# Clustered attention and a top-2 mixture of experts: the experts' first layer on float16 halves, scaled by powers of two found on the chip, with new first steps and a last list made by matmuls

## The chip, the cores and the metric

The program runs on one core of one Trainium2 chip. The metric is the device time of one execution in microseconds (us); the figure for a kernel is the median over its runs. The engines are TensorE (PE, with PEld for its weight loads), VectorE (DVE), ScalarE (ACT), GpSimd (POOL) and SyncE (SP, which here only sends DMAs).

## The reference, cut to what matters

```python
def _attn_ref(q, k, v, centroids):            # q, k, v: 4 x 8 x 768 x 64; centroids: 8 x 16 x 64
    q_n, k_n, c_n = (t / (norm(t) + 1e-06) for t in (q, k, centroids))
    q_assign = np.argmax(np.einsum('bhsd,hcd->bhsc', q_n, c_n), axis=-1)
    k_assign = np.argmax(np.einsum('bhsd,hcd->bhsc', k_n, c_n), axis=-1)
    mask = q_assign[:, :, :, None] == k_assign[:, :, None, :]
    scores = np.where(mask, q @ k.T / 8, -1e9)
    return softmax(scores) @ v

def _moe_ref(x, w_gate, w_noise, noise, w1, w2):   # x: 3072 x 512; w1: 8 x 512 x 1024; w2: 8 x 1024 x 512
    noisy_logits = x @ w_gate + np.log1p(np.exp(x @ w_noise)) * noise
    top2_w = softmax of the two largest, top2 their experts
    for e in range(8):
        for k in range(2):
            mask = top2[:, k] == e
            h = np.maximum(x[mask] @ w1[e], 0.0)
            out[mask] += top2_w[mask, k, None] * (h @ w2[e])
```

All inputs are float32; x is the attention's output, heads side by side.

## The kernel before, in words

**Attention.** 16 head pairs (4 batches of 4), each pair 12 steps: two heads, six blocks of 128 keys. A step makes scores of one block against 768 queries (`scores`, lines 485 and 486: matmuls into PSUM, then `Exp` on ACT), splits the weights into a bfloat16 upper part and a float16 rest (`split_p`, line 497, on POOL, in the last steps on DVE), and four steps later multiplies with v (`values`, lines 514 to 520, 16-bit matmuls with 65 or 64 columns). Queries and keys stand as an fp32r upper half and rest in two big tiles, `A` and `B`, three of each in turn. They are filled by DMAs from `hl` (`b_place`, line 426, ten a pair, 2.25 MB), with the one-hot cluster rows from `mk` (`b_mask`, four DMAs) and the negated row maximum from `nt` (`b_negT`). `b_max` (lines 454 and 457) finds the row maximum: 24 matmuls a pair, each with one DVE reduction out of PSUM. For pair 0 `nt` goes out once for each head, later once a pair.

**The order.** It is written by hand in `attention`: `at(step, f)` puts each function into a third of a step, and the table `AT` holds the steps. Within one engine's queue everything then runs in that order, so a function that waits holds up what stands behind it on its engine. SP sends nearly all loads and copies. PSUM has a ring of six buffers (`ps`).

**Experts.** After each batch the gate (`g_gate`) picks two experts a token and writes each token's number and weight to a list in DRAM by indirect DMAs (`g_list`, line 703, twelve a batch, on POOL). For each expert up to 832 rows (`CAP`, seven blocks of 128 or 64) are gathered by the list (`gather_x`), transposed (`turn_x`) and split into halves (`halves`, lines 905 and 906: ACT copies to the upper half, DVE subtracts for the rest). w1 and w2 are loaded through the staging tile `stg` (three buffers) and split alike. `layer1` (line 953) does for each of 8 blocks of F and 4 of D three matmuls (upper by upper, upper by rest, rest by upper), each over two parts of 416 columns: 192 matmuls an expert; `layer2` (line 992) does 24 matmuls of 512 columns a block of rows. For expert 0 the first four blocks of rows come from the lists of batches 0 to 2 alone (`lst0`, 512 columns); the other three (320 columns) wait for the last batch's list. All of layer 1 and 2 is fp32r.

Of the kernel before, what the change touches and what calls it, by code (L numbers as in the profile page):

```python
# [27 lines left out]
    first={'place': -2.333, 'sims': [-3.333, -2.667], 'sum': [-2.333, -2.333], 'max1': -2.333, 'ge': -2.333, 'max2': -2.333, 'eq': -1.333, 'mask': 1.667, 'bmask': 4.0, 'ky': -2.333, 'split': [-5.333, -5.0, -5.333, -4.0], 'bmax': [10.0, 17.0], 'neg': [17.667, 24.667], 'negT': [20.667, 27.667]},  # L28
    L=4, qk=-20.667, v=-8.667,
    vscale=-0.667, vsplit=10.667, vstep=1.0, split=[-4.667, -3.667, -4.0, -3.333], place=-0.667,  # L30
    sims=[-3.0, 2.0], sum=[2.333, 3.333], max1=3.333, ge=3.667, max2=4.333, eq=4.667, mask=5.667, bmask=6.0,
# [3 lines left out]
    vd=[1, 1, 2, 3, 4, 5], sec=-7.333, qf=-8.667,  # L35
    fv={'v': -2.333, 'vscale': -1.0, 'am': 0.0, 'amstep': 0.333, 'vsplit': 3.0, 'vstep': 2.0},
    thr=0.333, bsec=0.0)
# [6 lines left out]
class Kernel:  # L44
# [17 lines left out]
    def constants(self):  # L62
# [55 lines left out]

    def ps(self):
        return self.psum.tile([128, 512], F32, name="ring", bufs=6)  # L120

    def rnorm(self, n, r):
# [4 lines left out]
        nc.scalar.preload_act_table(AF.Exp)  # L127
# [5 lines left out]
    def centroids(self):  # L133
# [4 lines left out]
        nc.gpsimd.dma_start(c1, self.cent.rearrange("h c d -> (h c) d"))  # L138
# [7 lines left out]
    def c_turn(self):  # L146
# [4 lines left out]
        hi = self.pre.tile([128, HC], F32R, name="chi")  # L151
        lo = self.pre.tile([128, HC], F32R, name="clo")
        nc.scalar.activation(hi, p[:, :HC], AF.Copy)
        nc.vector.tensor_tensor(lo, p[:, :HC], hi, op=OP.subtract)
        for s in range(2):
            r = slice(64 * s, 64 * s + 64)
            for src, dst, c0 in ((hi, self.wh, 64 + 32 * s), (lo, self.wh, 80 + 32 * s)):
# [3 lines left out]
    def attention(self, ctx):  # L161
# [27 lines left out]
        for p in range(NP):  # L189
# [864 lines left out]
```

## Time and profile before

| | us |
|---|---|
| time, median of 3 runs | 1123.19 (1122.86 to 1123.75) |
| the profiled execution | 1116.65 |
| its span | 1114.9 |
| PE busy | 1056.4 (95%) |
| DVE, ACT, POOL busy | 612.7, 476.8, 559.2 |
| layer 1, PE (line 953, 1536 matmuls) | 290.3 |
| layer 2, PE (line 992, 1152 matmuls) | 273.7 |
| attention, end of the last values | some 482 |

The span is cut into the start (to about 60 us), the attention's steady steps, its end with the first expert's weights (440 to 482), the last gate and expert 0 (to some 560), and experts 1 to 7. PE is busy in nearly all of it, so the reading goes by where PE waits and by what each of its matmuls takes. A matmul's own duration in the trace holds its latency; what counts in a dense run is the distance from one start to the next, that is, busy time over count.

### The profile page before, as it was taken

Reading aid. Unit: us, or ns where it says so; the run is one execution under the profiler, and the core shown is the slowest. Engines: PE = TensorE matmul, PEld = TensorE weight load, DVE = VectorE, ACT = ScalarE, POOL = GpSimd, SP = SyncE. Lnnn points to the kernel's source line nnn. Section 1 sums busy time; section 2 is a strip of 40 time slices with the busy share of each in tenths; the row PEclk is TensorE's granted clock in tenths of the full one; section 3 lists DMA queues with packets and bytes.
Section 4 is the critical chain, followed back from the end, with each engine's and each line's share of the span. In section 5 each row is a group of like instructions: output and inputs, shape, how many; then the busy total and the mean of one; then the engine's idle time right before and its main releaser. Section 6 shows DMA issues by size and latency. Waiting matters only on the chain. (4 is left out here: it accounts for less than half of the span.)

```text
span 1114.9 us, 22318 instructions
## 1 busy us (share of the span) xinstructions
PE 1056.4 (95%) x8658; PEld 943.2 (85%) x8658; DVE 612.7 (55%) x1326; ACT 476.8 (43%) x961; POOL 559.2 (50%) x608
## 2 busy tenths in 40 slices
PE   4799999999999999889899999999999999999995
PEld 4589888888889888778889899898898898998983
DVE  5867786878687869964254333344244334433411
ACT  3476767676767675732233223133132232330300
POOL 4767775789678968606433351343233413522311
PEclk9899999999999999999899999999999999999998
DMA  8856767566757653132244342352153233523200
GB/s 232 179 140 153 176 157 203 143 171 156 206 143 178 155 151 106 39 135 82 86 126 157 133 136 78 126 176 84 67 168 125 94 112 134 161 68 106 76 32 32
DMA packets 87327, 144.46 MB, mean 130 GB/s; under 512 B 13945, under 2 KB 65529, under 8 KB 86706
## 3 DMA queue, kind: packets, MB, share of 16 engines
q1 hardware_dynamic: 71922, 106.45, 35.8%
q0 software_dynamic: 13712, 36.42, 9.7%
q8 instruction: 69, 1.13, 0.4%
q10 hardware_dynamic: 1584, 0.13, 0.1%
q14 instruction: 40, 0.33, 0.1%
HBM read 78.21 MB, written 26.53 MB: 94 GB/s over the span
## 5 line engine op out<-in xcount | busy, mean ns | idle before, releaser
L953 PE MATMUL ring<-xT,w1t 128*128 128x416 f32 (+2 forms) x1536 | 290.3, 350 | 0.0
L497 POOL TENSOR_TENSOR pl<-pe 128x768 f16<-128x768 f32 x173 | 252.2, 1473 | 72.3 <-ACT pe L486 69.5
L953 PEld LDWEIGHTS ring<-xT,w1t 128*128 128x128 f32 x1536 | 282.7, 188 | 6.6 <-DVE xT L906 0.3
L992 PE MATMUL ring<-w2t,hT 128*128 128x512 f32 x1152 | 273.7, 394 | 0.0
L992 PEld LDWEIGHTS ring<-w2t,hT 128*128 128x128 f32 x1152 | 214.5, 189 | 43.3
L486 ACT ACTIVATE pe<-ring,l 128x384 f32<-128x384 f32 x384 | 201.1, 578 | 54.2 <-PE ring L485 48.8
L1005 POOL DMA_INDIRECT out<-yo,lst x56 | 65.6, 1171 | 237.3 <-DVE yo L1001 187.5
L457 DVE TENSOR_REDUCE aux<-ring 128x1 f32<-128x384 f32 x192 | 108.0, 563 | 70.6 <-PE ring L454 66.0
L485 PE MATMUL ring<-A 128*128 128x384 f32 x384 | 141.3, 368 | 0.3 <-DVE aux L457 0.3
L963 DVE SCALAR_TENSOR_TENSOR hT<-ring,hT 128x416 fp32r<-128x416 f32 (+3 forms) x128 | 66.2, 554 | 124.1 <-ACT hT L962 124.1
L962 ACT ACTIVATE hT<-ring 128x416 fp32r<-128x416 f32 (+3 forms) x128 | 56.8, 488 | 181.0 <-PE ring L953 180.9
L932 POOL DMA_INDIRECT xg<-xs,lst x56 | 65.7, 1173 | 130.9 <-PE ring L943 105.1
L485 PE MATMUL ring<-B 128*128 128x384 f32 x384 | 129.4, 337 | 1.8 <-DMA B<-nt 1.8
L1001 DVE SCALAR_TENSOR_TENSOR yo<-ring,lst,xt 128x512 f32<-128x512 f32 (+1 forms) x49 | 36.7, 750 | 166.6 <-PE ring L992 145.8
L454 PE MATMUL ring<-A 128*128 128x384 f32 x384 | 110.5, 363 | 7.5 <-ACT pe L486 2.6
L905 ACT ACTIVATE xT<-ring 128x512 fp32r<-128x512 f32 (+1 forms) x56 | 31.0, 565 | 176.8 <-PE ring L943 176.8
L457 DVE TENSOR_REDUCE mm<-ring 128x1 f32<-128x384 f32 x192 | 105.2, 548 | 0.0
L514 PE MATMUL av<-vv,pe 128*128 128x65 f16 x1152 | 98.2, 196 | 4.5 <-DVE xt L528 4.4
L514 PEld LDWEIGHTS <-pe 128*128 128x128 bf16 x1152 | 80.5, 99 | 19.9 <-issue 11.8
L516 PE MATMUL av<-vv,pe 128*128 128x64 f16 x1152 | 97.2, 193 | 0.0
L454 PEld LDWEIGHTS ring<-A 128*128 128x128 f32 x384 | 71.0, 194 | 20.3 <-ACT pe L486 9.8
L516 PEld LDWEIGHTS <-pe 128*128 128x128 bf16 x1152 | 78.8, 99 | 0.3
(174 smaller groups left out, 1354.9 us busy)
## 6 DMA issues: line engine op xcount, KB each, us to landing
stg<-in_moe_w SPq DMA_DIRECT2D x64, 512.0 KB
A<-hl SPq DMA_DIRECT2D x30, 384.0 KB
B<-hl SPq DMA_DIRECT2D x30, 384.0 KB
vt<-in_v SPq DMA_DIRECT2D x8, 768.0 KB
out<-zt SPq DMA_DIRECT2D x12, 512.0 KB
xs<-xt SPq DMA_DIRECT2D x4, 1536.0 KB
A<-hl SPq DMA_DIRECT2D x60, 96.0 KB
B<-hl SPq DMA_DIRECT2D x30, 192.0 KB
```

The source lines that it names most:

```text
L454: nc.tensor.matmul(t, A[:, 0, s, j * 128:j * 128 + 128], A[:, 1, s, n * 384:n * 384 + 384], start=True, stop=True)
L457: nc.vector.tensor_reduce(o, t, axis=X, op=OP.max, negate=True)
L485: nc.tensor.matmul(t, M[:, 1 - qi, s, ks], M[:, qi, s, ns], start=not qi, stop=bool(qi))
L486: nc.scalar.activation(pe[:, n], t, AF.Exp, bias=self.l64[:, 0:1], scale=self.scale)
L497: (nc.vector if last else nc.gpsimd).tensor_tensor(lo, pe, hi, op=OP.subtract)
L514: nc.tensor.matmul(av[:, j, :], ph[:, js], vv[:, hh, kj, 64:129], start=(kc == 0 and j == 0), stop=False, skip_group_check=True)
L516: nc.tensor.matmul(av[:, j, :64], ph[:, js], vv[:, hh, kj, 0:64], start=False, stop=False, skip_group_check=True)
L932: self.nc.gpsimd.indirect_dma_start(out=xg[:r], out_offset=None, in_=self.xs[:n], in_offset=bass.IndirectOffsetOnAxis(ap=self.entry(e, t)[ ...
L953: nc.tensor.matmul(p, self.w1t[:, wi, c, f * 128:f * 128 + 128], self.xT[:, xi, c, n0:n1], start=(i == 0), stop=(i == 3 * ND - 1))
L963: nc.vector.scalar_tensor_tensor(h1, x, 0.0, h0, op0=OP.max, op1=OP.subtract)
L992: nc.tensor.matmul(p, self.hT[:, hi, f, t * 128:t * 128 + 128], self.w2t[:, wi, f], start=(i == 0), stop=(i == 3 * NF - 1))
L1005: i = nc.gpsimd.indirect_dma_start(out=self.out, out_offset=bass.IndirectOffsetOnAxis(ap=en[:r, 0:1], axis=0), in_=yo[:r], in_offset=None, ...
```

## The change

Four things, all in one diff.

1. `w1t` and `xT` become float16. Both are multiplied by a power of two first: the largest absolute value over all partitions is found on the chip (`x_max` from the maxima of v that the attention has anyway, `max_w1` for each expert), spread by a transpose, a maximum and a matmul with a row of constants (`scale_a`, `scale_b`), cut to its exponent by a bit mask, and its reciprocal scales both halves (`scaled_halves`). The product of the two powers (`ce`) is multiplied into the tokens' weights (`eff`, `weight`).
2. `stg` gets six buffers; w1 is loaded earlier (`prep_w1`), and its maxima are taken when it lands.
3. The last batch's list isn't written and read back: `upper`, `l_hot` and `l_sum` make it by one-hot comparisons and 12 float32 matmuls, added to what the earlier batches wrote (`lst`, now loaded sooner).
4. The first steps: other steps in `AT`, centroid halves written straight to `wh`, the loads of the second q and k and of v later, the gate's loads on SP, the `Exp` table after the first `nt`, and clears of `xg` on POOL.

```diff
-    first={... 'mask': 1.667, 'bmask': 4.0, ... 'bmax': [10.0, 17.0], 'neg': [17.667, 24.667], 'negT': [20.667, 27.667]},
+    first={... 'mask': -1.0, 'bmask': -1.0, ... 'bmax': [3.667, 22.667], 'bstep': [1.0, 0.667], 'neg': [9.0, 26.667], 'negT': [9.333, 27.333]},
-    vd=[1, 1, 2, 3, 4, 5], sec=-7.333, qf=-8.667,
-    fv={'v': -2.333, 'vscale': -1.0, 'am': 0.0, ...},
-    thr=0.333, bsec=0.0)
+    vd=[1, 1, 2, 3, 4, 5], sec=-6.0, qf=-4.0, place1=4.333,
+    fv=[{'v': -5.0, 'vscale': 13.0, 'am': 24.333, ...}, {'v': 9.0, 'vscale': 11.667, ...}],
+    thr=0.333, bmax1=14.667, bstep1=0.5)
...
-        nc.gpsimd.dma_start(c1, self.cent.rearrange("h c d -> (h c) d"))
+        nc.sync.dma_start(c1, self.cent.rearrange("h c d -> (h c) d"))
...
-        hi = self.pre.tile([128, HC], F32R, name="chi")
-        lo = self.pre.tile([128, HC], F32R, name="clo")
-        nc.scalar.activation(hi, p[:, :HC], AF.Copy)
-        nc.vector.tensor_tensor(lo, p[:, :HC], hi, op=OP.subtract)
...
-                nc.vector.tensor_copy(dst[r, :, c0:c0 + C],
-                                      src.rearrange("p (h c) -> p h c", c=C)[r])
+            nc.scalar.activation(hi, src, AF.Copy)
+            nc.vector.tensor_tensor(lo, src, hi, op=OP.subtract)
...
+        for i in range(2):
+            at(z - 45 + 2 * i, self.x_scale, i)
+            at(z - 13 + i, self.w1_scale, 0, i)
+        at(z - 46, self.x_max)
         for i in range(4):
-            at(z - 24 + i if i < 3 else z - 9, self.load_w1, 0, i)
+            at(z - 24 + i, self.load_w1, 0, i)
+            at(z - 19 + i, self.max_w1, 0, i)
             at(z - 10 + 2 * i, self.split_w1, 0, i)
...
-        self.w1t = self.mw.tile([128, 2, self.DM // 128, self.F], F32R, name="w1t")
+        self.w1t = self.mw.tile([128, 2, self.DM // 128, self.F], F16, name="w1t")
...
-        self.xT = mo.tile([128, 2, ND, CAP], F32R, name="xT")
+        self.xT = mo.tile([128, 2, ND, CAP], F16, name="xT")
...
-        for i in range(2 * NJ):
-            self.g_list(b, i)
+        self.l_hot(0)
         for i in range(4):
             if i >= 2:
                 self.load_w2(0, i)
-            self.split_w2(0, i)
             if f < NF:
                 self.layer1(0, f, [A])
                 f += 1
-        self.load_list(1)
+            if i < 2:
+                self.l_sum(i)
+            if i < 1:
+                self.l_hot(i + 1)
+            self.split_w2(0, i)
...
+    def l_hot(self, h):
+        self.hot = self.mo.tile([128, NJ, 128], F32, name="hot", bufs=1)
+        nc.vector.tensor_tensor(self.hot, self.low[:, NJ * h:NJ * h + NJ, None].to_broadcast([128, NJ, 128]),
+                                self.lower[:, None, :].to_broadcast([128, NJ, 128]), op=OP.is_equal)
+        self.ent = self.mo.tile([128, n, 2, 2, W], F32, name="ent", bufs=1)
...
+    def l_sum(self, h):
+        for i in range(NJ):
+            nc.tensor.matmul(self.lps, self.hot[:, i], ent[:, i], start=(h == 0 and i == 0), stop=(h == 1 and i == NJ - 1))
+        if h == 1:
+            nc.vector.tensor_tensor(self.idx, self.lps[:, :W], ls[:, :, 0], op=OP.add)
+            nc.vector.tensor_tensor(self.lsw, self.lps[:, W:], ls.bitcast(F32)[:, :, 1], op=OP.add)
...
+    def scaled_halves(self, dst, st, s):
+        self.nc.scalar.activation(dst[:, 0], st, AF.Copy, scale=s)
+        self.nc.vector.scalar_tensor_tensor(dst[:, 1], st, s, dst[:, 0], op0=OP.mult, op1=OP.subtract)
+    def scale_a(self, m):
+        nc.tensor.transpose(t[:k, :128], m, self.ident)
+        nc.vector.reduce_max(g[:k], t[:k, :128], axis=X)
+    def scale_b(self, g, f, p, s):
+        nc.tensor.matmul(t, f, g, start=True, stop=True)
+        nc.vector.tensor_scalar(p.bitcast(I32), t.bitcast(I32), 0x7F800000, None, op0=OP.bitwise_and)
+        nc.vector.reciprocal(s, p)
+    def max_w1(self, e, c):
+        self.nc.vector.tensor_reduce(self.wm[:, c:c + 1], self.stg[1, c], axis=X, op=OP.max, apply_absolute_value=True)
...
-        self.stg[1, c] = st = self.mw.tile([128, self.F], F32, name="stg", bufs=3)
+        self.stg[1, c] = st = self.mw.tile([128, self.F], F32, name="stg", bufs=6)
...
-            self.nc.vector.memset(xg, 0.0)
+            self.nc.gpsimd.memset(xg, 0.0)
```

How it moves instructions, at three places. Names of tiles are those of the program; after each comes the shape. First SP's queue near the start, before: the mask copies of pair 0 (`mk` into `A_142`), the copies of pair 1 (`xt` into `A_143` and `B_146`), its mask, a load of v, and the first `nt` of pair 0.

```order
L426 DMA A_142<-mk 16x2x384 x4
L426 DMA A_143<-xt 64x4x384
L426 DMA A_143<-xt 32x2x384 x2
L426 DMA B_146<-xt 64x4x384
L426 DMA B_146<-xt 32x4x384
L426 DMA A_143<-xt 64x4x384
L426 DMA A_143<-xt 32x2x384 x2
L426 DMA B_146<-xt 64x4x384
L426 DMA B_146<-xt 32x4x384
L426 DMA A_143<-mk 16x2x384 x4
L301 DMA vt<-in_v 128x4x384
L426 DMA B_145<-nt 2x6x128
```

And after, from the same mask copies (now into `A_151`): two loads of q and k, the first `nt`, then the copies of pair 1.

```order
L455 DMA A_151<-mk 16x2x384 x4
L323 DMA qk<-in_q 128x4x384
L323 DMA qk<-in_k 128x4x384
L455 DMA B_154<-nt 2x6x128
L455 DMA A_152<-xt 64x4x384
L455 DMA A_152<-xt 32x2x384 x2
L455 DMA B_155<-xt 64x4x384
L455 DMA B_155<-xt 32x4x384
L455 DMA A_152<-xt 64x4x384
L455 DMA A_152<-xt 32x2x384 x2
L455 DMA B_155<-xt 64x4x384
L455 DMA B_155<-xt 32x4x384
```

The first `nt` of pair 0 has moved from behind pair 1's copies and mask to ahead of them; the second `nt` of pair 0 stands behind pair 2's copies, as before.

Next PE's queue at the start, before, behind the sums of pair 0: the matmul that spreads v's maxima, then pair 1's transposes, then the mask's transposes (the one-hot tile `oh_148`).

```order
L388 MATMUL ring<-csum,sm 128x64 x6
L322 LDWEIGHTS vones
L322 MATMUL ring<-vm,vones 128x4
L323 LDWEIGHTS ones
L323 MATMUL ring<-tiny,ones 128x4
L352 MATMUL ring<-ident,qk 128x128 x12
L418 LDWEIGHTS oh_148
L418 MATMUL ring<-identb,oh_148 128x128
```

After:

```order
L417 MATMUL ring<-csum,sm 128x64 x6
L447 LDWEIGHTS oh_157
L447 MATMUL ring<-identb,oh_157 128x128
L447 LDWEIGHTS oh_157
L447 MATMUL ring<-identb,oh_157 128x128
```

The mask's transposes now follow the sums; v's maxima have gone behind the first scores, and pair 1's transposes behind the mask.

Last DVE's queue at the end of the attention, before: the row maxima of the last pair (`aux`, `mm`) and the splits of the attention weights that DVE takes over from POOL (`pl`).

```order
L457 TENSOR_REDUCE mm<-ring 128x1
L457 TENSOR_REDUCE aux<-ring 128x1
L457 TENSOR_REDUCE mm<-ring 128x1
L497 TENSOR_TENSOR pl<-pe 128x768
L457 TENSOR_REDUCE aux<-ring 128x1
L457 TENSOR_REDUCE mm<-ring 128x1
L497 TENSOR_TENSOR pl<-pe 128x768
```

After:

```order
L486 TENSOR_REDUCE mm<-ring 128x1
L1042 TENSOR_REDUCE wm<-stg 128x1
L486 TENSOR_REDUCE aux<-ring 128x1
L486 TENSOR_REDUCE mm<-ring 128x1
L1042 TENSOR_REDUCE wm<-stg 128x1
L526 TENSOR_TENSOR pl<-pe 128x768
L486 TENSOR_REDUCE aux<-ring 128x1
L486 TENSOR_REDUCE mm<-ring 128x1
L1042 TENSOR_REDUCE wm<-stg 128x1
```

Between them now stand the maxima of the first expert's w1 (`wm`), four in all.

## Rows read from the trace of the kernel before

**Rows 1.** The page: span, busy times, and DVE's tenths in 40 slices.

```profile
span 1114.9 us, 22318 instructions
PE 1056.4 (95%) x8658; PEld 943.2 (85%) x8658; DVE 612.7 (55%) x1326; ACT 476.8 (43%) x961; POOL 559.2 (50%) x608
...
DVE  5867786878687869964254333344244334433411
```

**Rows 2.** Windows: us, busy PE, PEld, DVE, ACT, POOL (instructions), PEclk, DMA share, GB/s.

```profile
0.00:20.00 20.00, 8.88 (x33) 7.66 (x33) 10.56 (x34) 5.56 (x10) 11.87 (x21) 1.00 0.93 264
20.00:30.00 10.00, 5.60 (x34) 5.08 (x34) 5.70 (x11) 4.94 (x10) 0.64 (x1) 1.00 0.55 126
30.00:40.00 10.00, 6.77 (x28) 5.62 (x28) 7.70 (x16) 3.76 (x7) 8.95 (x7) 0.66 0.88 172
40.00:60.00 20.00, 17.91 (x79) 12.73 (x79) 18.07 (x42) 7.79 (x17) 13.17 (x8) 0.91 0.87 202
...
440.00:450.00 10.00, 10.00 (x146) 9.19 (x145) 9.58 (x21) 6.35 (x13) 8.82 (x10) 1.00 0.02 3
...
530.00:540.00 10.00, 7.41 (x27) 6.00 (x28) 1.72 (x3) 1.58 (x3) 3.18 (x6) 0.66 0.25 95
```

**Rows 3.** Groups by shape, layer 1 on PE: count, busy us, mean ns, idle before.

```profile
L953 PE MATMUL ring<-xT,w1t 128*128 128x416 f32 x1344 | 253.7, 350 | 0.0
...
L953 PE MATMUL ring<-xT,w1t 128*128 128x512 f32 x96 | 22.3, 391 | 0.0
...
L953 PE MATMUL ring<-xT,w1t 128*128 128x320 f32 x96 | 14.2, 309 | 0.0
```

**Rows 4.** Timeline of PE: start us, us, line, operation, shapes, count.

```profile
62.84 0.35 PE L520 MATMUL av<-vv,pl 128*128 128x65 f16 x6
...
63.57 0.50 PE L418 MATMUL ring<-identb,oh 128*128 128x128 bf16 x6
...
729.37 6.92 PE L953 MATMUL ring<-xT,w1t 128*128 128x416 f32 x36
```

**Rows 5.** Groups by shape: the 16-bit weight loads of line 520.

```profile
L520 PEld LDWEIGHTS <-pl 128*128 128x128 f16 x1152 | 48.0, 98 | 0.0
```

**Rows 6.** Groups by shape: the nearest rows for what is added.

```profile
L497 POOL TENSOR_TENSOR pl<-pe 128x768 f16<-128x768 f32 x173 | 252.2, 1473 | 72.3 <-ACT pe L486 69.5 <-PE av L520 1.8
...
L457 DVE TENSOR_REDUCE aux<-ring 128x1 f32<-128x384 f32 x192 | 108.0, 563 | 70.6 <-PE ring L454 66.0
...
L388 PE MATMUL ring<-csum,sm 128*128 128x64 f32 x192 | 26.4, 277 | 1.6 <-ACT sm L378 1.6
...
L311 DVE TENSOR_REDUCE vm<-vt 128x2 bf16<-128x768 f32 x16 | 14.9, 943 | 0.0
...
L931 DVE MEMSET xg<- 128x512 f32 x4 | 1.9, 485 | 0.2
```

**Rows 7.** Waits of PEld, 400 to 570 us: total, times, longest.

```profile
PEld L514 <- DVE xt L528: 5.5, 3, 3.7
```

**Rows 8.** Timeline around the wait for gathered rows.

```profile
532.59 2.58 PE L943 MATMUL ring<-ident,xg 128*128 128x128 f32 x12 [3.54 <-DMA xg<-xs,lst]
...
535.10 7.24 PE L992 MATMUL ring<-w2t,hT 128*128 128x512 f32 x24
```

**Rows 9.** Timeline of the first steps, all engines.

```profile
21.20 0.56 DVE L409 TENSOR_TENSOR oh<-ring,km 128x384 bf16<-128x384 f32 x1
...
26.22 0.57 PE L418 MATMUL ring<-identb,oh 128*128 128x128 bf16 x6
...
30.45 2.93 SPq L426 DMA_DIRECT2D A<-xt  x3
...
41.05 3.60 SPq L426 DMA_DIRECT2D A<-mk  x4
...
60.18 0.67 SPq L426 DMA_DIRECT2D B<-nt  x1
...
65.76 0.45 PE L485 MATMUL ring<-B 128*128 128x384 f32 x1 [1.46 <-DMA B<-nt]
```

More of the change, by code (lines that the diff above doesn't have):

```diff
@@ L321, in total @@
             T["t"] = self.ps()[:, :4]
[L322 removed]
+            nc.tensor.matmul(T["t"], self.vones, self.vm[:, 2 * b + g], start=True, stop=False)
             nc.tensor.matmul(T["t"], self.ones, self.tiny, start=False, stop=True)
@@ L727, in entry, with weight @@
     def entry(self, e, t):
-        return self.lst0[:, t] if e == 0 and t < self.TA else self.lst[:, e, t]
+        i = e * self.T + t
+        return self.lst0[:, t, 0:1] if e == 0 and t < self.TA else self.idx[:, i:i + 1]
+    def weight(self, e, t):
+        return self.we[e % 2][:, t:t + 1]
     def rows(self, t):
@@ L815, in tail @@
         if n < E:
-            for i in range(3):
-                self.load_w1(n, i)
             if e == 0:
@@ L832, in tail @@
             if n < E:
-                if t == t0:
-                    self.split_w1(n, 0)
-                    self.load_w1(n, 3)
-                if t == t0 + 1:
-                    for i in range(1, 4):
+                if e:
+                    self.prep_w1(n, t - t0 + 5)
+                for i in range(4):
+                    if t == t0 + (max(i, 1) if e else min(i, 1)):
                         self.split_w1(n, i)
@@ L857, in extra @@
         with tc.If(self.more > 0):
+            for j in range(self.NJ):
+                for k in range(2):
+                    nc.gpsimd.indirect_dma_start(
+                        out=self.tbl, out_offset=bass.IndirectOffsetOnAxis(ap=self.addr[:, j, k:k + 1], axis=0),
+                        in_=self.rec[:, j, k, :], in_offset=None)
             with tc.For_i(0, E) as e:
@@ L860, in extra @@
                     self.load_w1(e, i)
+                    self.max_w1(e, i)
+                for i in range(2):
+                    self.w1_scale(e, i)
+                for i in range(4):
                     self.split_w1(e, i)
@@ new lines, in w1_scale, with eff @@
+    def w1_scale(self, e, i):
+        if i == 0:
+            self.wg_ = self.scale_a(self.wm)
+        else:
+            self.pw1, self.sw1 = (self.mw.tile([128, 1], F32, name=n, bufs=1) for n in ("pw1", "sw1"))
+            self.scale_b(self.wg_, self.fw, self.pw1, self.sw1)
+            self.ce = self.mw.tile([128, 1], F32, name="ce", bufs=2)
+            self.nc.vector.tensor_tensor(self.ce, self.pw1, self.px, op=OP.mult)
+    def eff(self, e, t0, t1):
+        if t0 == 0:
+            self.we[e % 2] = self.mw.tile([128, self.T], F32, name="we", bufs=2)
+        w = self.lst0.bitcast(F32)[:, t0:t1, 1] if e == 0 and t1 == self.TA else self.lsw[:, e * self.T + t0:e * self.T + t1]
+        self.nc.vector.tensor_scalar(self.we[e % 2][:, t0:t1], w, self.ce, None, op0=OP.mult)
@@ L996, in layer2 @@
         en = self.entry(e, t)
-        wt = en.bitcast(F32)[:r, 1:2]
+        wt = self.weight(e, t)[:r]
         if e == 0:
```

135 lines of the change are left out of this document (107 added, 28 removed).

## The prediction

> **What bounds the kernel now.** I read the page first: of a span of 1114.9 us TensorE (PE) is busy for 1056.4 [rows 1], so a gain must come from PE's own work or from the stretches in which it has none. The windows show where those lie [rows 2]: in the first 60 us PE is busy for 8.88 + 5.60 + 6.77 + 17.91 = 39.2 us, so it stands idle for 20.8, and its granted clock falls to 0.66 in one stretch. There the DMA engines are 55 to 93% busy, and in 40 to 60 us VectorE (DVE) works 18.07 of 20 us. A second hole lies at 530 to 540 us (PE 7.41 of 10, clock 0.66). Before the experts DVE is the full engine (9.58 of 10 us at 440 to 450). Behind 540 us PE never waits, so a nanosecond off a matmul there is a nanosecond off the end, and work added on ACT, DVE or POOL there is free as long as it fits beside PE.
>
> **Layer 1 on float16.** The groups by shape [rows 3] give PE time for each matmul: 253.7 us/1344 = 188.8 ns at 416 columns, 22.3/96 = 232.3 at 512, 14.2/96 = 147.9 at 320. At the full clock of 2.4 GHz the columns alone are 173.3, 213.3 and 133.3 ns, so each fp32r matmul carries 14 to 19 ns above its columns. A run of 36 says the same, (6.92 - 0.35)/35 = 187.7 ns [rows 4]. The 16-bit matmuls of the attention show what is left of that: six with 128 columns take (0.50 - 0.22)/5 = 56 ns, 2.7 above their 53.3; six with 65 columns take (0.35 - 0.19)/5 = 32 ns, 5 above their 27.1 [rows 4]; each has a weight load of its own ahead of it, and that load's 98 ns [rows 5] don't show in the spacing. No wide 16-bit matmul is in the trace, so I bound it: at best 2.7 above the columns, at worst as now. I take 3.5, near the rows with a load for each matmul: 176.8, 216.8, 136.8 ns. Gain: 12.0 x 1344 = 16.1 us, 15.5 x 96 = 1.5, 11.1 x 96 = 1.1, together **-18.7 us** (-19.5 to 0). Number and width of the matmuls stay.
>
> The Trainium skill's page "TensorE: Matmul & The Clock Gate" (Weight-path perf modes) has a fast weight load that 128 columns of a type other than FP32 get and FP32 doesn't; by that the 14 ns would be load time and go, which makes the same sum as mine, and the trace has only the narrow matmuls to show it.
>
> **Scales.** Each expert's w1, and x once, gets a transpose and a float32 matmul with one column: 9 pairs. The nearest float32 rows are the sums of line 388, two records for each matmul, 26.4/192 = 0.137 us a record [rows 6]. Three records a pair: 27 x 0.137 = **+3.7 us** on PE (1 to 6). What the answers need (maximum, bit mask, reciprocal on DVE) stands one list of matmuls ahead, so I cost PE's wait at nothing in the experts; if that cover failed, some 0.5 us each. The w1 maxima there, 4 an expert at about 0.943 x 1024/768 = 1.26 us [rows 6], lie on a DVE that is busy for three to five tenths of nearly every slice there (the last row of [rows 1]); the changed splits keep their number. w1 is fetched earlier into six buffers in place of three, so its loads have more time.
>
> **End of the attention.** Here the cover fails. The order of DVE shows four maxima of w1 between the row maxima of the last head pair: 4 x 1.26 = 5.0 us, and seven small operations, about 1.1, where DVE was 96% busy [rows 2]. Four clears of 0.485 us [rows 6] leave DVE for POOL, which only writes there: -1.9. Net 4.2 us, and PE in that stretch already waits for DVE for 5.5 us [rows 7]. DVE's own gaps can take little: **+3.5 us** (0 to 6). Queued behind a maximum are the row maxima, whose PSUM buffers PE needs.
>
> **The last list by matmuls.** Now PE waits 3.54 us for gathered rows that come of twelve list writes on POOL, a list load and a gather; then it runs cold: 12 transposes take 2.58 us and the 24 matmuls behind them 7.24 [rows 8]. At 232.3 ns the 24 are 5.6 + 0.2, so 1.5 is lost there, and of the 2.58 about half (1.3). All 6.3 us go, as the new chain gives indices before layer 2 begins, one list of 72 matmuls ahead of their use. In their place come 12 float32 matmuls of 112 columns, 24 records: 3.3 us at 0.137, up to twice that as they have more columns than 64; I take 3.5. The first six need a comparison of 672 and one of 768 elements (DVE, about 0.9 us each by its maxima of 768) and four POOL products of 168 elements, 1.47 x 168/768 = 0.32 each and a fixed part [rows 6]: some 3.3 us behind the addresses, with one layer 1 pass of 2.6 us for cover but hidden only in part, since DVE also evicts. I take a wait of 1.9. Sum: -6.3 + 3.5 + 1.9 = **-0.9 us** (-4 to +3).
>
> **First steps.** In the order, the mask of head pair 0 now follows its sums at once; before, its transposes began at 26.22 though the one-hot rows were done at 21.20 + 0.56 = 21.8 [rows 9]. With the centroids written straight into place (2 to 3 us of casts gone, of which I take 1.7, since the same DVE also makes the splits) they begin near 20.1, and SP sends the mask at some 21.8, 6 us sooner. Maxima of the first half only: 12 reductions of 0.563 us [rows 6] from about 26 us, so the first `nt` goes out near 33.5 and the first scores start some 9 us earlier than now. But SP is in order, and now this `nt` stands ahead of pair 1's copies: those took from 30.45 to 41.05, 10.6 us at a DMA share of 0.87 or more, and the mask 3.6 [rows 2, 9]. So: pair 1's copies 34.2 to 44.8, mask to 48, pair 2's copies to 58.6, and only then the second half's `nt`, sent at 60.18 now. It lands now at 65.76, behind two loads of q and k that SP sends just ahead of it; these follow it in the new order, so I give it 3 us: 61.6. PE blocks on it at step 6, as now. Gain 65.8 - 61.6 = 4.2, less four maxima matmuls put off: **-4 us**. Ends: -9 if the copies are not held by bandwidth, +2 if the `nt` takes as long as before. The gate's loads, moved from ACT's queue to SP's, stand ahead of pair 3's copies, which wait for PE anyway: about 2.7 us by the 0.9 of a mask copy, nine steps before use, nothing.
>
> **How the numbers follow.** -18.7 + 3.7 + 3.5 - 0.9 - 4.0 = -16.4 us. The profiled execution took 1116.65 (1114.9 of span), 6.5 under the median of the runs, 1123.2; I take the difference from the median: 1106.8, said as **1106.5**.
>
> **Rivals.**
> (1) The start is freed: copies overlap more than I think, -9 in place of -4, and the list gains its 4: 1096 to 1101. For it speaks the idle 20.8 us; against, the DMA shares.
> (2) The start gives nothing and DVE's maxima cost 6: 1112 to 1119. SP's order speaks for it.
> (3) Slower: the weight load, now an instruction of its own, is not hidden behind a wide matmul. Then 128 columns are added to each: (416 + 128)/2.4 = 226.7 ns, +37.9 x 1344 = +50.9; 512 columns +34.4 x 96 = 3.3, 320 columns +38.8 x 96 = 3.7. With the other terms (+2.3) the time is 1183. It decides from 12 ns of unhidden load a matmul. Against it: 32 and 56 ns spacing with loads between [rows 4, 5]. The same page of the Trainium skill (Part 3, The mechanism) says that loads overlap running matmuls only in other row groups, which would be this case; the trace does not agree, with 32 ns.
> (4) The 14 ns are not the type's: layer 1 stays, 1123.2 + 2.3 = 1125.5.
> (5) 16-bit pairs go faster than a column a cycle. If 512 columns took 131 ns and 416 106.4, layer 1 would lose (188.8 - 106.4) x 1344 = 110.7 and 16 on the others: 999. No row of the trace has a matmul under its columns at 2.4 GHz. That 131 is the figure of the Trainium skill, same page, "Back-to-back issue gap", for a stream of load and matmul; the rows here side with the other formula there, columns/2.4 plus 2.5 ns.
> That the type is not changed at all I leave out: the tiles of x and w1 are declared float16, and the order lists loads apart from matmuls.
>
> **Chances.** Forecast (1101 to 1112) 0.60; (1) 0.17; (2) 0.13; (3) 0.04; (4) 0.04; (5) 0.02. Within 0.2% is 2.2 us, about what a measurement of this kernel tells from no change. Faster: 0.60 + 0.17 + 0.12 + 0.02 = 0.91; same 0.03 (the tail of 2 and half of 4); slower 0.06. The range 1096 to 1116 takes in the forecast, most of (1) and two thirds of (2).
>
> **What would show it.** Layer 1 groups at 176 to 178 ns for 416 columns (right) or 188 and 227 (4, 3); no PE wait for gathered rows at 530 us; DVE over 95% and PE waits for it at 440 to 480; PE's wait for `nt` of the second half near 61 us. The prediction is wrong if layer 1's PE time is not near 271 us, or if PE's idle time in the first 60 us changes by more than 9.

## The result, and the profile after

| | before | after |
|---|---|---|
| median of 6 runs each, taken together | 1123.03 (1120.22 to 1123.75) | 1112.04 (1107.88 to 1112.76) |
| the profiled execution, its span | 1116.65, 1114.9 | 1111.9, 1110.1 |
| layer 1, PE | 290.3 | 274.4 |

The ratio is 0.9891 (0.9872 to 0.9910): the kernel is 11.0 us faster, and 5.5 us slower than forecast. In a later series on one chip the ratio was 0.9934 (0.9918 to 0.9949), 1110.89 against 1118.45. There the kernel before, unchanged, had a median 4.6 us lower than here, and the kernel after one about 1 us lower; the last section shows what the profiles have of it.

The page's first lines and groups of PE by shape (group, operation, shapes, count, busy time and mean ns, idle time before); they answer [rows 1, 3, 6]:

```profile
span 1110.1 us, 22397 instructions
...
PE 1044.8 (94%) x8709; PEld 815.9 (74%) x8709; DVE 660.2 (59%) x1412; ACT 484.3 (44%) x962; POOL 542.2 (49%) x598
...
L1105 PE MATMUL ring<-xT,w1t 128*128 128x416 f16 x1344 | 237.7, 339 | 0.2 <-DVE xT L1010 0.2
...
L1105 PE MATMUL ring<-xT,w1t 128*128 128x512 f16 x96 | 23.1, 400 | 0.0
...
L1105 PE MATMUL ring<-xT,w1t 128*128 128x320 f16 x96 | 13.6, 299 | 0.0
...
L1029 PE MATMUL ring<-gmax,fw 4*128 4x1 f32 x16 | 3.0, 256 | 0.0
...
L1020 PE MATMUL ring<-ident,wm 128*4 128x128 f32 x8 | 2.3, 289 | 2.0 <-DVE wm L1042 2.0
```

The 416 columns are 0.1 ns off the forecast of 176.8: 237.7 / 1344 = 176.9 ns. The scales' two lines are 5.3 us, and 6.0 with x's own pair.

Windows of after, answering [rows 2]:

```profile
0.00:20.00 20.00, 9.03 (x43) 8.12 (x44) 11.46 (x35) 5.35 (x11) 18.97 (x26) 0.94 0.78 211
20.00:30.00 10.00, 8.35 (x36) 7.47 (x34) 6.54 (x14) 3.18 (x7) 5.93 (x4) 0.61 0.84 228
30.00:40.00 10.00, 5.03 (x29) 4.83 (x29) 7.92 (x17) 4.28 (x7) 0.00 (x0) 0.73 0.49 99
40.00:60.00 20.00, 15.84 (x109) 12.55 (x107) 16.26 (x37) 10.44 (x21) 10.77 (x9) 0.97 0.87 187
...
456.00:460.00 4.00, 0.48 (x2) 0.51 (x3) 3.90 (x8) 0.24 (x1) 3.53 (x6) 0.73 0.03 3
460.00:464.00 4.00, 4.00 (x35) 3.50 (x35) 3.26 (x9) 2.59 (x5) 3.33 (x6) 0.50 0.05 8
...
500.00:520.00 20.00, 17.85 (x99) 9.30 (x97) 14.28 (x46) 5.12 (x9) 5.53 (x9) 0.91 0.15 56
530.00:540.00 10.00, 10.00 (x48) 8.27 (x47) 0.94 (x2) 0.00 (x0) 2.16 (x4) 1.00 0.14 54
```

PE's idle time in the first 60 us is 60 - 38.25 = 21.8, where it was 20.8: the holes of the start have not closed. The hole at 530 is gone, and a new one stands at 456 to 460, with the granted clock at its lower level (0.50, that is 1.2 GHz) behind it. PE's longest waits from 440 to 560 us (engine, tile and line, what it waited for, total, times, longest) name the places; `nm` is the negated row maximum of the last pair, `xt` the attention's output, `wm` the maxima of w1, `hot` the one-hot rows of the list:

```profile
PE ring L500 <- DVE nm L495: 4.2, 1, 4.2
PE av L543 <- DVE xt L557: 2.9, 2, 1.8
PE ring L1020 <- DVE wm L1042: 2.0, 1, 2.0
PE ring L761 <- DVE hot L745: 1.8, 1, 1.8
```

The second was there before, and longer; the waits for `wm` and `hot` are new, and that for `nm` was 1.3:

```profile
PE av L514 <- DVE xt L528: 4.4, 2, 3.4
```

Starts of the same matmuls in the profiles, in us, read from timelines of PE ("again" is a later profile; "float16 alone" and "no scales" are experiments below):

| | scores 0 | step 6, behind `nt` | step 30 | step 164 | step 184 | layer 1 | its 320 columns | expert 1 | last matmul |
|---|---|---|---|---|---|---|---|---|---|
| before | 49.5 | 65.8 | 116.6 | 427.8 | 462.8 | 490.2 | 542.2 | 574.1 | 1101.0 |
| before, again | 50.3 | 66.1 | 117.0 | 428.8 | 470.1 | 494.8 | 546.7 | 578.6 | 1105.5 |
| after | 41.9 | 62.0 | 117.5 | 429.3 | 470.4 | 495.2 | 546.6 | 580.1 | 1095.1 |
| after, again | 41.9 | 62.1 | 117.1 | 428.3 | 469.6 | 494.5 | 544.5 | 578.0 | 1093.1 |
| float16 alone, again | 50.4 | 66.1 | 117.0 | 430.7 | 465.6 | 494.0 | 541.7 | 572.6 | 1083.6 |
| no scales, again | 41.0 | 61.7 | 115.3 | 426.9 | 461.8 | 485.9 | 537.2 | 568.1 | 1079.5 |

### The profile page after: what moved, and what is told of

Read it like the earlier page. It is cut to its first block, busy times and chain, and to the rows that moved or that the text cites. A ratio compares the mean times of both kernels' runs of the same rounds, so it can differ in the third digit from the quotient of the medians.

```text
span 1110.1 us, 22397 instructions
## 1 busy us (share of the span) xinstructions
PE 1044.8 (94%) x8709; PEld 815.9 (74%) x8709; DVE 660.2 (59%) x1412; ACT 484.3 (44%) x962; POOL 542.2 (49%) x598
## 4 chain that ended last, share of the span: by engine, by line
PE 72%; DVE 11%; issue 8%; POOL 2%; ACT 2%; DMA 2%; SPq 1%; POOLq 0%; DVEq 0%; ACTq 0%
PE ring L1105 20%; PE ring L1144 19%; PE ring L514 9%; PE ring L483 5%; PE av L543 3%; PE av L549 2%; PE av L545 2%; PE ring L1095 2%; DVE aux L486 2%; PE ring L402 2%; PE ring L381 2%; DMA A<-mk 1%; DVE mm L486 1%; PE ring L417 1%; POOL out L1157 1%
## 5 line engine op out<-in xcount | busy, mean ns | idle before, releaser
L1105 PE MATMUL ring<-xT,w1t 128*128 128x416 f16 (+2 forms) x1536 | 274.4, 340 | 0.2 <-DVE xT L1010 0.2
L1105 PEld LDWEIGHTS <-w1t 128*128 128x128 f16 x1536 | 149.9, 98 | 121.8 <-issue 5.4
L1157 POOL DMA_INDIRECT out<-yo,idx x52 | 62.8, 1208 | 233.6 <-DVE yo L1153 144.3
L1153 DVE SCALAR_TENSOR_TENSOR yo<-ring,we,xt 128x512 f32<-128x512 f32 (+1 forms) x49 | 36.8, 750 | 156.5 <-PE ring L1144 133.7
L1115 DVE SCALAR_TENSOR_TENSOR hT<-ring,hT 128x416 fp32r<-128x416 f32 (+3 forms) x128 | 66.1, 553 | 80.3 <-ACT hT L1114 74.4
L1084 POOL DMA_INDIRECT xg<-xs,idx x52 | 54.2, 1041 | 116.8 <-PE ring L1095 100.3
L1009 ACT ACTIVATE xT<-ring,sx 128x512 f16<-128x512 f32 (+1 forms) x56 | 35.7, 653 | 150.5 <-PE ring L1095 150.5
```

Source lines behind the costliest of these rows:

```text
L1105: nc.tensor.matmul(p, self.w1t[:, wi, c, f * 128:f * 128 + 128], self.xT[:, xi, c, n0:n1], start=(i == 0), stop=(i == 3 * ND - 1))
L1115: nc.vector.scalar_tensor_tensor(h1, x, 0.0, h0, op0=OP.max, op1=OP.subtract)
L1157: i = nc.gpsimd.indirect_dma_start(out=self.out, out_offset=bass.IndirectOffsetOnAxis(ap=en[:r], axis=0), in_=yo[:r], in_offset=None, boun ...
```

## Experiments

Each was timed beside the kernel before, in three series: (S1) before 1123.8, (S2) before 1117.87 on another chip, (S3) before 1118.45 on the chip of S1. The kernel after itself was timed in the first comparison and in S3 alone, so what S1 and S2 say of it compares across series. An issue gap is idle time of PE in which it waits for nothing that the profile shows. Theories: T1, the terms of the prediction; T2, float16 alone gives all of the gain and the scaling that it needs eats a large part; the first steps give nothing.

**Float16 alone.** The kernel before with

```diff
-        self.w1t = self.mw.tile([128, 2, self.DM // 128, self.F], F32R, name="w1t")
+        self.w1t = self.mw.tile([128, 2, self.DM // 128, self.F], F16, name="w1t")
-        self.xT = mo.tile([128, 2, ND, CAP], F32R, name="xT")
+        self.xT = mo.tile([128, 2, ND, CAP], F16, name="xT")
```

> The kernel before with one thing changed: w1t and xT are float16 (no scaling, so the rests lose low bits; nothing else is left out). Theory A (the spacing of the columns): layer 1's PE time falls from 290.3 to 271 us and the kernel is 18 to 19 us quicker than before, 1104 to 1105; no rest of the kernel moves. Theory B (as the trace of after shows, 274.4): some 16 us, 1107, where a cold clock in expert 0 eats the gain of the 512 and 320 columns. Theory C: half or less, under 9 us, because the quicker layer 1 meets its evictions or loads and waits.

Measured in S1: 1105.10, 18.7 us less than before, ratio 0.9838 (0.9812 to 0.9864).

> The kernel before with float16 alone (no scaling), again, now beside the others. Against the kernel without scales it lacks the new first steps, the list by matmuls and the earlier loads of w1. Theory A: first steps 0, list 1.0: 1 us slower than the kernel without scales. Theory B: as the prediction, first steps 4 and list 0.9: 5 us slower. Theory C: its end of the attention, as that of the kernel before, has PE's issue gaps and the half clock behind them in most executions, which the kernel without scales has not shown: 5 to 7 us slower, all of it between step 180 and step 184.

Measured in S3: 1099.06, 19.4 less, 0.9824 (0.9808 to 0.9841). Layer 1's groups of that run:

```profile
L953 PE MATMUL ring<-xT,w1t 128*128 128x416 f16 x1344 | 237.6, 339 | 0.0
...
L953 PE MATMUL ring<-xT,w1t 128*128 128x512 f16 x96 | 21.0, 379 | 0.0
...
L953 PE MATMUL ring<-xT,w1t 128*128 128x320 f16 x96 | 13.2, 299 | 0.0
```

That is 176.8, 218.8 and 137.5 ns and 271.8 us in all, where 271 was forecast; both series agree with theory A of the first expectation. With the type the layer's weight loads became shorter, from 188 to 98 ns each (before, then after):

```profile
L953 PEld LDWEIGHTS ring<-xT,w1t 128*128 128x128 f32 x1536 | 282.7, 188 | 6.6 <-DVE xT L906 0.3
L1105 PEld LDWEIGHTS <-w1t 128*128 128x128 f16 x1536 | 149.9, 98 | 121.8 <-issue 5.4
```

In after the 512 columns have 23.1 us, since some of them run at the lower clock behind the wait for `hot` at 510 us; after, again has the same wait without the lower clock, and 21.4.

**No scales.** The kernel after with `x_max`, `max_w1`, `scale_a`, `scale_b` gone and

```diff
-        self.scaled_halves(self.w1t[:, :, c], self.stg[1, c], self.sw1)
+        self.halves(self.w1t[:, :, c], self.stg[1, c])
```

> The kernel after with all scaling left out: no maxima, no transposes and matmuls of the scales, halves without a factor. What stays of the change is float16, the list by matmuls, the first steps and the earlier loads of w1. Theory A (prediction): scales 3.7 + end of attention 3.5 = 7 us quicker than after, 1105. Theory B (trace of after): nine pairs of 0.66 us, a wait of 2.0 in expert 0 and the end of the attention with 0.5 to 3.6: 8.5 to 11.5 quicker, 1101 to 1104. Theory C: the same as the kernel with float16 alone, 1105, since list and first steps give nothing.

> The kernel after with all scaling left out, again, now beside the kernel after on one chip. Theory A (the prediction's terms for scales and end of attention, 3.7 + 3.5): 7 us quicker than after. Theory B (sum of the marks in the traces: end of the attention 5.6 to 6.8, expert 0 2.7, six further pairs 0.6 each): 12 to 13 us quicker than after.

> The kernel after, unchanged, so that it stands on one chip beside the three runs that follow. Expected: 1112 within 2 us, and the same marks in the trace (PE waits 4.2 us for nm near 455, with the half clock behind it; 1.8 for hot near 510; 2.0 for wm near 555).

Measured: no scales 1098.46 in S2 (0.9838, 0.9812 to 0.9864) and 1097.25 in S3 (0.9812, 0.9796 to 0.9828); after, again 1110.89. So in one series the scaling costs 13.6 us: T2 holds, a little above B's 12 to 13. (In S2 the near copy of after with expert 1's w1 sooner stands 11.3 above no scales.) The prediction's terms for the scaling were 3.7 and, with the clears left out, 5.4, together 9.1; the 7 us of theory A are the terms net of the clears, which this kernel keeps. Where they lie is read from the table, after, again less no scales, again: 1.8 us at step 30 and 1.4 at step 164, 7.8 at step 184, 8.6 at layer 1, 7.3 at its 320 columns, 9.9 at expert 1, 13.6 at the end. So 7.2 lie at the end of the attention, 2.6 in expert 0's 320 columns (the wait of 2.0 and one pair) and 3.7 in the six pairs that follow, 0.6 each. The 1.8 at step 30 stand before any scaling, and the 1.3 that are lost between layer 1 and the 320 columns are none either: of these two profiles the one has the lower clock behind `nt` and the other behind `hot` (see the last section), and the two nearly cancel.

The kernel without scales is 1.8 us quicker than float16 alone in S3, with intervals that overlap (nearest to theory A of float16 alone, again; the gaps of its theory C did not come): first steps, list, clears and earlier loads of w1 together bring that, where 6.8 had been forecast (4 + 0.9 + 1.9).

**Without expert 0's maxima.** The kernel after; `wm` is set by a constant:

```diff
-            at(z - 19 + i, self.max_w1, 0, i)
+            at(z - 19 + i, self.no_max, i)
```

> The kernel after without the four maxima of expert 0's w1; a constant takes their place, so their work is left out; the transpose and matmul of its scale stay. Theory A (the prediction's term): the maxima cost 3.5 us at the end of the attention; PE's wait of 4.2 us for nm falls to 1.3 and the kernel is 3 to 4 us quicker than after. Theory B: without that wait PE's issue gaps of 0.44 us come back there (six of them between 459 and 466 us in the second trace of the kernel before, with a clock of 0.57 behind them), and the kernel gains under 1.5 us.

Measured in S2: 1106.13, 0.9914 (0.9890 to 0.9938); the kernel after stood at 0.9934 in S3 against almost the same before. By the ratios that is 2.2 us less, by the medians 4.8, across two chips, and the intervals overlap; the traces say more. This one, against that of after, is 0.9 us ahead at step 176 and 6.5 at step 184: 5.6 us for four maxima of 1.21. Nor is it one profile against one: from step 176 to 184 the five profiles with the maxima between the row maxima take 18.7 to 19.8 us, and the three without maxima 13.3 to 13.9. The wait for nm and the windows behind it:

```profile
PE ring L500 <- DVE nm L495: 1.3, 1, 1.3
```

```profile
456.00:460.00 4.00, 3.95 (x67) 3.37 (x66) 3.90 (x11) 2.69 (x6) 3.46 (x6) 1.00 0.06 10
460.00:464.00 4.00, 4.00 (x68) 3.52 (x68) 2.47 (x4) 3.71 (x8) 3.45 (x6) 1.00 0.02 1
```

The wait accounts for 4.2 - 1.3 = 2.9. Most of the rest is clock: from step 176 to 180 PE is busy for 9.2 us in after and 6.9 here with the same 94 matmuls; after has a granted 0.73, 0.50 and 0.92 in 456 to 468 us, this run 1.00 throughout. Theory A, with a larger price; no issue gaps came.

**Maxima behind the row maxima.** The kernel after with

```diff
-            at(z - 13 + i, self.w1_scale, 0, i)
+            at(z - 12.667 + i, self.w1_scale, 0, i)
-            at(z - 19 + i, self.max_w1, 0, i)
+            at(z - 15.333 + i * 0.667, self.max_w1, 0, i)
```

> The kernel after, with the four maxima of expert 0's w1 taken right behind the last row maximum of the attention instead of between the row maxima (steps -15.3 to -13.3 from the end in place of -19 to -16, the scale one step part later). Theory A: what the maxima cost is their place; the row maximum of the last pair is done some 5 us sooner, PE's wait of 4.2 us for nm falls to about 1.3, and 2.5 to 3.6 us of the end of the attention come back: 0.25 to 0.3 percent quicker than after. Theory B: DVE is full in that stretch whatever the order, the wait moves to the split weights or the values, and the time stays as after within 1 us.

Measured in S1: 1113.52, 0.9919 (0.9894 to 0.9944), no gain. PE's waits from 440 to 500 us:

```profile
PE ring L1020 <- DVE wm L1042: 5.5, 1, 5.5
...
PE ring L500 <- DVE nm L495: 1.3, 1, 1.3
```

The wait for nm went as A said, and the transpose of the scale, which I had left just behind the maxima in PE's own queue, took over with 5.5. The time fits neither A's gain nor B's 1 us, and the run does not tell them apart.

**Maxima sooner, gate's loads later, expert 1's w1 sooner.** Nothing left out:

```diff
-        at(z - 26, self.open_weights)
+        at(z - 29.667, self.open_weights)
-            at(z - 24 + i, self.load_w1, 0, i)
-            at(z - 19 + i, self.max_w1, 0, i)
+            at(z - 29.333 + 0.667 * i, self.load_w1, 0, i)
+            at(z - 26.667 + i, self.max_w1, 0, i)
-        at(10.667, self.load_gate)
+        at(18.0, self.load_gate)
...
-            self.prep_w1(1, f)
+            if f < 3:
+                self.prep_w1(1, f + 2)
+            if 5 <= f < 7:
+                self.w1_scale(1, f - 5)
```

> The kernel after with three things moved, nothing left out: expert 0's w1 is loaded and its maxima are taken about seven steps sooner, before the last row maxima; the gate's loads on SP go behind pair 3's copies (step 18 in place of 10.7); expert 1's w1 comes two blocks sooner and its scale stays where it is. Theory A: each price was one of place. PE's wait for nm falls from 4.2 to 1.3 and 3.5 to 6 us come back at the end of the attention; pair 3's copies leave SP 1.7 us sooner and PE is 1 to 1.6 us earlier from step 24 on; the wait for wm of 2.0 goes: together 6 to 9 us quicker than after. Theory B: DVE is as full where the maxima go (0.85 to 0.93 busy), so 2 to 4 us of the 5 are lost there again, and pair 3 waits for PE, not for SP: 2 to 4 us quicker than after.

Measured in S3: 1107.90, 0.9902 (0.9884 to 0.9920), 3.0 us quicker than after: B. The wait for nm fell to 1.3, but where the maxima now stand PE waits for row maxima four times:

```profile
PE ring L514 <- DVE aux L486: 2.3, 4, 0.9
```

```profile
440.00:444.00 4.00, 2.69 (x43) 2.11 (x40) 3.71 (x9) 1.49 (x3) 2.60 (x2) 1.00 0.00 0
444.00:448.00 4.00, 3.18 (x29) 2.25 (x29) 3.51 (x11) 1.05 (x4) 0.36 (x2) 1.00 0.00 0
```

Against after, again it loses 4.0 us between steps 168 and 176 and wins 5.7 between 176 and 180; 1.4 of 5.6 remain from step 164 to layer 1. In neither of the two places tried had DVE room for them. Moving the gate's loads behind pair 3's copies gives nothing: from step 12 to 24 this run takes 27.2 us, after, again 26.7. The wait for wm in expert 0 is gone, and 1.9 us with it (1.3 behind at the 320 columns, 0.6 ahead at expert 1).

**Expert 1's w1 sooner, scale too.** As above for w1 alone, with `prep_w1(1, f + 2)` for all f, so that the scale moves along:

> The kernel after with expert 1's w1 loaded, and its maxima taken, two blocks sooner (from the third block of expert 0's layer 2 on), so that its scale has the cover that the other experts have. Theory A: PE's wait of 2.0 us for wm at 555 us goes and nothing takes its place: 2 us quicker than after. Theory B: the loads meet those of w2 or the maxima delay evictions: within 0.7 us of after.

Measured in S2: 1109.79, 0.9939 (0.9919 to 0.9959), not to be told from after's 0.9934. That is near B's time, but not for B's reason: the wait fell only to 1.4, since the scale's transpose again follows the last maximum at once. Against the run above, it is the distance between maxima and transpose that counts.

```profile
PE ring L1022 <- DVE wm L1044: 1.4, 1, 1.4
```

**Old first steps.** The kernel after with the table, centroid copies and queues of before:

```diff
+    vd=[1, 1, 2, 3, 4, 5], sec=-7.333, qf=-8.667,
+    fv={'v': -2.333, 'vscale': -1.0, 'am': 0.0, 'amstep': 0.333, 'vsplit': 3.0, 'vstep': 2.0},
...
-        at(-13, self.exp_table)
-        at(10.667, self.load_gate)
```

> The kernel after with the first steps of the kernel before: its table of steps, the gate's loads on ACT's queue, centroid copies, Exp table and queue of the centroid load as before. Theory A (the prediction): the new first steps gain 4 us, so this kernel is 4 us slower than after. Theory B (the two traces): the new first steps are 7.5 us ahead at the first scores, 1.5 at step 7 and 1 to 1.5 behind from step 24 on, so this kernel is 1 to 1.5 us quicker than after. Theory C: the traces' before was a quick execution and the new start is worth 5 or more, so this kernel is over 5 us slower.

Measured in S1: 1112.25, 0.9901 (0.9878 to 0.9924), where after in the first comparison had 1112.04 and 0.9891: between A and B, the first steps are worth 0.2 us, nothing that can be measured. The rows at step 6 of this run, then of after:

```profile
64.98 0.42 PE L519 MATMUL ring<-A 128*128 128x384 f32 x1
66.42 0.44 PE L519 MATMUL ring<-B 128*128 128x384 f32 x1 [1.01 <-DMA B<-nt]
```

```profile
58.92 0.33 PE L514 MATMUL ring<-A 128*128 128x384 f32 x1
62.00 0.69 PE L514 MATMUL ring<-B 128*128 128x384 f32 x1 [2.74 <-DMA B<-nt]
...
63.12 0.84 PE L483 MATMUL ring<-A 128*128 128x384 f32 x2
63.77 0.86 PE L447 MATMUL ring<-identb,oh 128*128 128x128 bf16 x6
```

**Old list.** The kernel after with the last batch's list written to DRAM and read back:

```diff
-        self.l_hot(0)
+        for i in range(2 * NJ):
+            self.g_list(b, i)
...
-            if i < 2:
-                self.l_sum(i)
-            if i < 1:
-                self.l_hot(i + 1)
```

> The kernel after with the last batch's list written and read back as in the kernel before (twelve indirect writes, list load, gather), no l_hot, no l_sum. Theory A (the prediction): the list by matmuls is worth 0.9 us, so this kernel is 0.9 us slower than after. Theory B: it costs more than it saves: its two waits and the cold matmuls behind them (1.8 us of wait, 1.8 of a cold clock, 2.7 of matmuls in the trace of after) stand against 6.3, and the cold clock at 530 us was there in one trace only; this kernel is 1 to 3 us quicker than after. Theory C: the wait for gathered rows at 530 us has grown with the quicker layer 1, so this kernel is 2 to 4 us slower.

Measured in S2: 1111.98, 0.9967 (0.9947 to 0.9987), by the medians 1.1 us above after in S3 and by the ratios 3.7; five of its twelve runs lie at 1115.07 to 1119.89, the other seven at 1109.58 to 1112.16, so that A and C can't be told apart. PE waits 4.9 us for gathered rows:

```profile
PE ring L1086 <- DMA xg<-xs,lst: 4.9, 2, 4.8
```

From the start of layer 1 to its 320 columns this run takes 52.4 us and the kernels with the list by matmuls 50.0 to 51.4. But float16 alone, which also has the old list, takes 49.7 and 47.7. So in this kernel the list by matmuls is worth 1 us or more; beside float16 alone the old one is 0.3 to 3.7 us quicker, and why its wait is shorter there (2.7) stays open.

**The kernel before, again.**

> The kernel before, unchanged. The profiled execution before took 1116.65 us, the median of the runs 1123.03; in the two traces the kernel after is only 4.8 us shorter in span, by the medians 11.0. Theory A: the profiled execution before was a quick one; its span follows the mean granted clock, and executions of this kernel lie between about 1115 and 1122 of span with the clock falling from 0.986 towards 0.98. Then the span of a typical one is some 1121, and the stretch in which it is longer shows a low clock or a wait. Theory B: the executions are alike in span (1115 within 1 us) and 6 us lie outside the span in the timed ones; then this run's spans are 1115 and its times 1121 to 1123.

Measured in S1: 1122.84 (1120.37 to 1123.95), span of the profile 1119.4: A as to the span, but the time doesn't follow the mean granted clock (1123.95 us at 0.985, 1121.20 at 0.979). It is 0.9 us behind the first profile at step 180 and 7.4 at step 184. PE's rows from there:

```profile
459.99 0.19 PE L514 MATMUL av<-vv,pe 128*128 128x65 f16 x1 [0.45 <-issue]
...
460.72 0.19 PE L516 MATMUL av<-vv,pe 128*128 128x64 f16 x1 [0.41 <-issue]
...
461.48 0.23 PE L520 MATMUL av<-vv,pl 128*128 128x65 f16 x2 [0.44 <-issue]
```

```profile
460.00:464.00 4.00, 2.50 (x27) 1.61 (x26) 0.96 (x1) 0.86 (x2) 3.35 (x7) 1.00 0.02 1
464.00:468.00 4.00, 3.17 (x30) 2.77 (x31) 1.64 (x2) 3.02 (x6) 0.43 (x1) 0.57 0.01 0
```

Here PE waited for nothing that the profile shows, seven times in 5.6 us, and ran at a granted 0.57 behind it. The first profile of before has no such row.

## Why the prediction was right, and where its sum was off

The time lies in the range and the sign is right; what came true is rival (2), the start that gives nothing and maxima that cost 6 (1112 to 1119), to which I gave 0.13. The terms are judged in S3. There float16 alone, which has the old end of the attention, shows no issue gaps, and neither does the profile that the terms were read from: 1110.89 - 1118.45 = -7.6, and the sum said -16.4. It splits there into float16 alone -19.4, scaling +13.6, all the rest -1.8.

That the forecast came within 5.5 us all the same is in part luck, since two errors had opposite signs. The gain was 8.8 us too large; but it was taken from 1123.2, where the median of S3 is 1118.45, and the difference of 6.5 between the median and the profile was carried over to the new kernel as if it were fixed. By the profiles a good part of it lies in the gaps: from step 164 to layer 1 before, again takes 3.6 us more than the first profile, and float16 alone in S1 5.0 more than in S3, and no profile of the new kernel has them. (That the timed runs have the gaps too is an inference; they leave no trace.)

- **Layer 1, -18.7: right.** -18.7 and -19.4 measured alone. The step held that took the narrow 16-bit matmuls (2.7 and 5 ns above their columns) for the wide ones: 3.5 above 173.3. (The best end of the range is 19.9 by its own 2.7 ns, not 19.5.) The Trainium skill's page "TensorE: Matmul & The Clock Gate" (Weight-path perf modes) has the fast weight load for types other than FP32. The trace agrees as far as the loads go, 188 and 98 ns; that the 14 ns were load time is not shown by it. The 131 ns of the same page of the Trainium skill ("Back-to-back issue gap") are not seen: 512 columns take 218.8. Part 3 of that page of the Trainium skill (The mechanism) has it that a load overlaps running matmuls only where its row group differs. That isn't seen either: each matmul here has its own load, and rival (3) would have shown 226.7 ns at 416 columns.
- **Scales, +3.7: too small.** The step that failed is the price of three records a pair at 0.137: the rows of line 388 which it was taken from stand in runs of equal matmuls, and here two records of 0.19 us of busy time and one of 0.29 make 0.66 a pair. Nine pairs are 6.0. And PE's wait, costed at nothing, came at one place, expert 0's 320 columns: four maxima of 1.21 between evictions, and the transpose right behind the last, 2.0.
- **End of the attention, +3.5: right as a net, for two errors that offset each other.** From step 164 to layer 1 the first profile of before takes 62.4 us, after 65.9 and after, again 66.2: +3.5 and +3.8. But no scales, again takes 59.0 there, so the scaling costs 7.2 and not 5.4, and the rest of the change gives 3.4 and not 1.9. In the first of the two the count of DVE time was right: nm is done at 459.4 in place of 454.3, and 1.5 of these 5.1 the kernel was behind already at step 176. What the step left out is the clock: a wait of 4.2 us ended with matmuls at the lower level until some 465 us. In the second, clears on POOL and earlier loads of w1 act together; float16 alone, again takes 63.3 us, so by this pair of profiles they give 4.3, all of it behind step 184. There PE waits for `xt` for 4.4 us in it and for 2.6 in no scales, again, and the granted clock from 478 to 486 us is 0.58 and 0.56 in the one and 1.00 in the other; which of the two changes did it was not separated. The 5.5 us which the prediction reads from [rows 7] are the weight loads' wait; PE's own was 4.4.
- **List, -0.9: open.** It costs 1 us or more to undo it in after, yet beside float16 alone the old list is quicker, and the medians resolve neither. The hole at 530 us is gone as forecast, a wait of 1.78 was forecast as 1.9, and the twelve matmuls take 3.1 us for 3.5. What was not in the sum is the clock behind the wait, and it doesn't always come: the twelve matmuls of 512 columns that follow, 2.6 us at 218.8 ns each, took 4.43 in after and 2.75 in after, again. PE's rows there, of both:

```profile
511.06 1.61 PE L761 MATMUL ring<-ent,hot 128*128 128x112 f32 x12 [1.78 <-DVE hot L745]
512.46 4.43 PE L1105 MATMUL ring<-xT,w1t 128*128 128x512 f16 x12
...
510.31 1.56 PE L761 MATMUL ring<-ent,hot 128*128 128x112 f32 x12 [1.78 <-DVE hot L745]
511.71 2.75 PE L1105 MATMUL ring<-xT,w1t 128*128 128x512 f16 x12
```

- **First steps, -4: wrong.** What was forecast up to the second half's `nt` came within some 1.5 us of its place: it was used at 62.0 (61.6 forecast; 61.6 to 62.5 in nine profiles with the new start, 65.8 to 67.3 in five with the old). The step that failed is the last, from that mark to the end. The mean lead of the nine over the five is 4.3 us there, 3.1 at step 7, 2.2 at step 12 and 0.9 at steps 24 and 30. A first part, up to step 12, goes because the work behind the wait isn't the same: from `nt` to step 12 PE has 170 matmuls with the new start and 160 with the old. Six of the ten are the one-hot transposes of the next pair, which with the old start are done before `nt` comes (at 63.57 in [rows 4], at 63.77 above with the new start); four are matmuls for row maxima. They cost 1.6 us; in three of the nine profiles, after among them, a further 1.3 to 1.5 is lost to a granted 0.50 from 62 to 64 us. After and, for comparison, the run without expert 0's maxima:

```profile
62.00:64.00 2.00, 2.00 (x8) 1.69 (x9) 0.32 (x1) 1.16 (x2) 0.00 (x0) 0.50 1.01 368
...
62.00:64.00 2.00, 1.45 (x15) 1.30 (x16) 0.45 (x1) 0.91 (x2) 0.23 (x1) 1.00 0.95 278
```

  A second part goes between steps 12 and 24, which take 26.9 us with the new start and 25.5 with the old. There, from 66 to 118 us, PE in after has two waits that before has not:

```profile
PE ring L483 <- ACT pe L515: 1.1, 1, 1.1
PE ring L483 <- DMA A<-mk: 0.8, 1, 0.8
```

  Most of it is step 21, which takes 2.4 to 3.0 us in the nine profiles and 1.7 in the five. There stands the second wait, for pair 3's mask. SP's queue says what holds the mask in after (three rows of SP, then ACT's, which makes the mask):

```profile
92.00 0.38 SPq L331 DMA_DIRECT2D vt<-in_v  x1
92.42 0.64 SPq L580 DMA_DIRECT2D tbl<-lg  x1
93.15 2.65 SPq L455 DMA_DIRECT2D A<-mk  x4
...
91.10 0.99 ACT L449 ACTIVATE mk<-ring,ms 128x768 fp32r<-128x768 bf16 x1 [0.45 <-PE ring L447]
```

  The mask is ready at 92.1 and goes out at 93.15, behind a load of v that waits 4.6 us for POOL's last split of v (done at 92.0; 85.3 in before, again). In before, again that load has gone out at 88.3, and the mask goes as soon as it is ready. No run moved v's splits, so this is read from the queue and not tested. The gate's loads moved behind the mask do not shorten the step: it takes 3.0 there, and the profile puts the wait down to one of them. PE's idle time in the first 60 us, 21.8 for 20.8, says the same as the sum.

## What to carry to other kernels

Price a transfer that comes sooner by the engine's idle time before and after, not by the moment at which one wait ends: an engine that arrives earlier has more of its work still to do. Look for the lower clock behind each wait on TensorE, and in more than one execution: here it came behind each of five waits of 4.2 us, and behind four of nine of 1.8. Check a forecast term by term even where the sum fits; here two pairs of errors offset each other. And when a cheaper data type needs a scale, time the type alone first: here it gives 19 us, its maxima and scales take 13.6 back, and half of that lies in the one stretch where VectorE was full.

## What the runs showed that was not expected

The kernel before, the same program, has a median of 1123 in the first comparison and in S1, 1118 in S2 and S3, and S1 and S3 ran on the same chip. The profiles show what may differ: with issue gaps of mostly 0.41 to 0.45 us on PE near 459 to 466 us (before, again, and float16 alone in S1) steps 180 to 184 take 11.9 and 10.9 us, without them (the first profile of before, float16 alone in S3) 5.4. No profile of a kernel with the new end of the attention has such gaps there; those without maxima ran only in S2 and S3, so whether they would have them is open. What holds PE there stays open.

The lower clock follows PE's waits at several places, at some of them not in every execution of the same code. Behind the 4.2 us for nm it comes in all five profiles that have this wait, behind the gaps (0.57) in both. At the second half's `nt` the three profiles with a wait of 2.6 to 2.7 have it, and four with 1.4 to 1.6 do not. Behind the 1.8 us for `hot` it comes in four of nine (after, maxima sooner, and no scales twice). Two profiles of one kernel can differ by 1 to 1.5 us for this alone, as much as several of the differences above.
